# A layer of LayerNorm, S5 scan and gated MLP, re-tiled into four 512-token chunks and ordered by a list scheduler inside the kernel

## The chip, the cores and the metric

One core of a Trainium2 chip. Times are device microseconds (us) of one execution. The kernel before takes 243.13 us (median of two runs, 241.75 to 244.52). A profiled execution gives a *span*, from the first to the last instruction. Engines: PE (TensorE, with its weight loads as PEld), DVE (VectorE), ACT (ScalarE), POOL (GpSimd), and SP, which here only issues DMAs.

## The reference

```python
def reference(A_x, A_Lambda_re, A_Lambda_im, A_B_re, A_B_im, A_C_re, A_C_im, A_log_dt, A_Dskip,
              B_x, B_w_gate, B_w_up, B_w_down):
    x  = A_x                                   # (1, 2048, 448), bfloat16
    xn = _layernorm(x)                         # no scale, no shift
    s  = S5(xn)                                # Bu = xn B_bar^T (complex); h_t = Lam_bar h_{t-1} + Bu_t
                                               # s = 2 Re(h C^T) + xn * Dskip ;  448 states
    g  = silu((sigmoid(xn Wg) * (xn Wu)) Wd)   # 448 -> 1792 -> 448
    return x + s * g
```

(The scan runs over all 2048 tokens.) The feature size 448 is 3 x 128 + 64. TensorE contracts over up to 128 rows, so every contraction over 448 features has a piece of 64 rows. Two 64-row matmuls can run side by side, one in the upper and one in the lower half of the array: a *pair*.

## The kernel before

Tokens are taken in chunks of up to 512 (the first and the last are of 256). Each gate/up unit of 128 hidden features does three full 128-row matmuls for the gate, three for the up half, and one pair for the two 64-row rests. So the array changes its tiling mode in each unit. ScalarE takes the two 512-column PSUM banks out by one instruction each.

```python
def unit_mms(banks, n, xnT, fulls, halves, half_first):
    ...
    def do_full():
        for i in range(nb):
            for kt in range(KF):                       # KF = 3, 128 rows each
                nc.tensor.matmul(banks[i][:, 0:n], lhsT=fulls[i](kt), rhs=xnT[:, kt, 0:n], ...)
    def do_half():
        for i in range(nb):
            lo = H if (i == 1 and ROWPAIR) else 0      # H = 64: upper or lower half of the array
            nc.tensor.matmul(banks[i][:, 0:n], lhsT=halves[i], rhs=xnT[lo:lo + H, 3, 0:n], ...)

def gu_unit(c, xnT, ft, half_first):
    ...
    nc.scalar.activation(sig[:, 0:n], gu[:, 0, 0:n], ACT.Sigmoid)
    nc.scalar.copy(out=ub[:, 0:n], in_=gu[:, 1, 0:n])
    nc.vector.tensor_tensor(out=hF, in0=sig[:, 0:n], in1=ub[:, 0:n], op=ALU.mult)
```

All large loads are issued by SP; ACT issues three tiny ones. B and C are transposed by PE, x of the first chunks by PE and of the later ones by DMA. The order of the instructions is written by hand ("weave" and "slots").

## Time and profile before

| | before |
|---|---|
| timed, median | 243.13 us |
| profiled span | 238.9 us |
| busy PE / DVE / ACT / POOL | 204.5 / 179.4 / 127.4 / 36.3 us |
| first gate/up matmul | 10.85 us |

The page's busy times and its slices (each digit is a fortieth of the span, in tenths busy; PEclk is the granted TensorE clock in tenths, so 5 is half speed and 9 is full; GB/s is what the DMA engines moved):

```profile
PE 204.5 (86%) x1146; PEld 98.1 (41%) x1160; DVE 179.4 (75%) x444; ACT 127.4 (53%) x254; POOL 36.3 (15%) x102
PE   7589538697974999989739999999999999999990
PEclk9889955999998999999959999999999999999997
GB/s 133 351 277 272 348 27 0 4 0 0 44 23 25 0 19 0 0 44 22 22 41 0 25 0 19 0 65 1 19 19 3 19 0 19 22 21 21 22 0 40
```

What PE waited for (engine, tile, line, what released it: us in total, times, longest):

```profile
PE bu L425 <- DMA xnT<-xn: 10.1, 2, 5.7
PE tpx L226 <- DVE xn L211: 8.9, 6, 4.9
```

PE is the engine that sets the time: 86% busy, and solid in the last third. The losses are in the first two thirds: waits for the transposed normalised x (`xnT`, `xn`), and after each wait the clock digit 5, in which the same work takes twice as long.

### The profile page before, as it was taken

Reading aid. Unit: us, or ns where it says so; the run is one execution under the profiler, and the core shown is the slowest. Engines: PE = TensorE matmul, PEld = TensorE weight load, DVE = VectorE, ACT = ScalarE, POOL = GpSimd, SP = SyncE. Lnnn points to the kernel's source line nnn. Section 1 sums busy time; section 2 is a strip of 40 time slices with the busy share of each in tenths; the row PEclk is TensorE's granted clock in tenths of the full one; section 3 lists DMA queues with packets and bytes.
Section 4 is the critical chain, followed back from the end, with each engine's and each line's share of the span. In section 5 each row is a group of like instructions: output and inputs, shape, how many; then the busy total and the mean of one; then the engine's idle time right before and its main releaser. Section 6 shows DMA issues by size and latency. Waiting matters only on the chain.

```text
span 238.9 us, 3346 instructions
## 1 busy us (share of the span) xinstructions
PE 204.5 (86%) x1146; PEld 98.1 (41%) x1160; DVE 179.4 (75%) x444; ACT 127.4 (53%) x254; POOL 36.3 (15%) x102
## 2 busy tenths in 40 slices
PE   7589538697974999989739999999999999999990
PEld 2246316343431444433314444344444455555550
DVE  7999179998799999999995792799666369533204
ACT  3468713478891736676703563874546273533232
POOL 2010720482000068830000000000000000000000
PEclk9889955999998999999959999999999999999997
DMA  6999900000211000011110000020000000000001
GB/s 133 351 277 272 348 27 0 4 0 0 44 23 25 0 19 0 0 44 22 22 41 0 25 0 19 0 65 1 19 19 3 19 0 19 22 21 21 22 0 40
DMA packets 15608, 11.75 MB, mean 49 GB/s; under 512 B 6083, under 2 KB 14662, under 8 KB 15590
## 3 DMA queue, kind: packets, MB, share of 16 engines
q1 hardware_dynamic: 15536, 11.41, 17.2%
q0 software_dynamic: 48, 0.11, 0.4%
q8 instruction: 9, 0.15, 0.3%
q14 instruction: 9, 0.07, 0.1%
q10 hardware_dynamic: 6, 0.00, 0.0%
HBM read 8.37 MB, written 1.84 MB: 43 GB/s over the span
## 4 chain that ended last, share of the span: by engine, by line
PE 48%; DVE 28%; DMA 10%; ACT 5%; POOL 3%; issue 3%; SPq 2%; DVEq 0%; POOLq 0%
PE gu L419 16%; PE acc L586 14%; PE acc L594 6%; DVE wv L517 6%; DMA wk<-in_B_w_gate_dram 5%; PE bu L419 5%; PE gu L425 3%; DMA bc<-in_A_C_im_dram 3%; DMA xnT<-xn 2%; DVE z L510 2%; DVE ta L506 2%; DVE hF L456 2%; DVE tb L508 1%; DVE hT L536 1%; DVE td L534 1%
## 5 line engine op out<-in xcount | busy, mean ns | idle before, releaser
L451 ACT ACTIVATE sig<-gu 128x512 bf16<-128x512 f32 (+1 forms) x56 | 30.4, 543 | 44.8 <-PE gu L425 34.5
L419 PE MATMUL gu<-xnT,wg 128*128 128x512 bf16 (+1 forms) x201 | 47.0, 340 | 2.9 <-ACT ub L455 1.2
L419 PE MATMUL gu<-xnT,wu 128*128 128x512 bf16 (+1 forms) x207 | 48.1, 340 | 0.2
L586 PE MATMUL acc<-wd,hF 128*128 128x448 bf16 x224 | 47.4, 357 | 0.9 <-DVE hF L456 0.8
L456 DVE TENSOR_TENSOR hF<-sig,ub 128x512 bf16<-128x512 bf16 (+1 forms) x56 | 21.0, 385 | 22.9 <-ACT ub L455 22.6
L586 PEld LDWEIGHTS <-hF 128*128 128x128 bf16 x224 | 22.3, 99 | 22.8 <-issue 2.0
L455 ACT CAST ub<-gu 128x512 bf16<-128x512 f32 (+1 forms) x56 | 29.6, 528 | 0.0
L419 PEld LDWEIGHTS <-wu 128*128 128x128 bf16 x210 | 20.8, 99 | 16.4 <-DMA wu<-in_B_w_up_dram 0.2
L419 PEld LDWEIGHTS <-wg 128*128 128x128 bf16 x210 | 17.6, 98 | 23.6 <-issue 12.9
L419 PE MATMUL bu<-xnT,bT 128*128 128x512 bf16 (+1 forms) x103 | 23.9, 367 | 0.7 <-ACT bus_606 L476 0.7
L425 PE MATMUL gu<-xnT,wk 64*128 64x512 bf16 (+1 forms) x140 | 21.2, 343 | 1.3 <-DMA wk<-in_B_w_up_dram 0.6
L594 PE MATMUL acc<-cT,hT 128*128 128x448 bf16 x98 | 20.8, 352 | 0.0
L600 ACT ACTIVATE sigd<-acc 128x448 bf16<-128x448 f32 x16 | 8.7, 544 | 16.1 <-PE acc L586 16.1
L425 PE MATMUL bu<-xnT,bT 64*128 64x512 bf16 (+1 forms) x35 | 7.1, 350 | 11.5 <-DMA xnT<-xn 10.1
L419 PEld LDWEIGHTS <-bT 128*128 128x128 bf16 x105 | 9.8, 104 | 13.0 <-issue 7.1
L594 PEld LDWEIGHTS <-hT 128*128 128x128 bf16 x112 | 11.0, 98 | 10.1
L216 POOL COPY xn<-xn 128x64 bf16<-128x64 bf16 x10 | 4.3, 426 | 70.8 <-ACT xn L215 70.8
L604 DVE TENSOR_TENSOR g_t<-zb,sigd 128x448 bf16<-128x448 bf16 x16 | 6.1, 384 | 11.4 <-ACT zb L602 11.4
L425 PEld LDWEIGHTS <-wk 64*128 64x128 bf16 x140 | 5.2, 94 | 14.3 <-issue 12.6
L226 PE MATMUL tpx<-ident,xn 128*128 128x128 bf16 x24 | 3.3, 279 | 8.9 <-DVE xn L211 8.9
L610 DVE TENSOR_TENSOR sg<-acc,g_t 128x448 bf16<-128x448 f32 x14 | 8.6, 618 | 2.6 <-PE acc L594 2.4
L170 DVE BATCH_NORM_STATS2 stats<-x_all 128x6 f32<-128x448 bf16 x16 | 9.7, 608 | 0.0
(269 smaller groups left out, 299.2 us busy)
## 6 DMA issues: line engine op xcount, KB each, us to landing
out_dram<-o_t SPq DMA_DIRECT2D x16, 112.0 KB, 1.7
wd<-in_B_w_down_dram SPq DMA_DIRECT2D x1, 1568.0 KB, 9.3
x_all<-in_A_x_dram SPq DMA_DIRECT2D x3, 448.0 KB, 7.8
wg<-in_B_w_gate_dram SPq DMA_DIRECT2D x1, 960.0 KB
wu<-in_B_w_up_dram SPq DMA_DIRECT2D x1, 960.0 KB, 11.1
wg<-in_B_w_gate_dram SPq DMA_DIRECT2D x1, 384.0 KB, 5.5
wu<-in_B_w_up_dram SPq DMA_DIRECT2D x1, 384.0 KB, 6.4
bc<-in_A_B_re_dram SPq DMA_DIRECT2D x1, 336.0 KB, 10.7
```

The lines of the kernel that those rows point to most:

```text
L170: nc.vector.bn_stats(out=stats[:], in_=x_all[:, t0 + i, :])
L419: nc.tensor.matmul(banks[i][:, 0:n], lhsT=fulls[i](kt), rhs=xnT[:, kt, 0:n], start=(kt == 0 and not half_first), stop=(kt == KF - 1 and ha ...
L425: nc.tensor.matmul(banks[i][:, 0:n], lhsT=halves[i], rhs=xnT[lo:lo + H, 3, 0:n], start=half_first, stop=not half_first)
L451: sg_ins = nc.scalar.activation(sig[:, 0:n], gu[:, 0, 0:n], ACT.Sigmoid).ins
L455: nc.scalar.copy(out=ub[:, 0:n], in_=gu[:, 1, 0:n])
L456: anchors["hF"] = nc.vector.tensor_tensor(out=hF, in0=sig[:, 0:n], in1=ub[:, 0:n], op=ALU.mult).ins
L517: V.tensor_tensor_scan(out=cell["wv"][:, k, 0:n], data0=rb, data1=cell["z"][:, k, 0:n], initial=(st[pt][:, k, :] if c else 0.0), op0=ALU.m ...
L586: nc.tensor.matmul(dacc[:, 0:D], lhsT=hFs[c][:, ft, j * P:(j + 1) * P], rhs=wd[:, ft, :], start=(ft == 0), stop=(ft == FT - 1))
L594: nc.tensor.matmul(y[:, 0:D], lhsT=hTs[c][:, hm, j * P:(j + 1) * P], rhs=K["cT"][:, cm, :], start=False, stop=(i == 6))
L600: nc.scalar.activation(sigd[:], dacc[:, 0:D], ACT.Sigmoid, scale=half)
L604: nc.vector.tensor_tensor(out=g_t[:], in0=zb[:], in1=sigd[:], op=ALU.mult)
L610: nc.vector.tensor_tensor(out=sg[:], in0=y[:, 0:D], in1=g_t[:], op=ALU.mult)
```

## The change

A rewrite. Its intent: every contraction over 448 features of gate and up becomes seven 64-row pairs, upper half into one PSUM bank and lower half into another, with no full 128-row matmul between, so a step of 14 matmuls has one tiling mode and fills two banks that ScalarE takes out with one 1024-column instruction. There are four chunks of 512 tokens. B, C and the later x chunks are transposed by DMA. And the program order of every engine comes from a small list scheduler in the kernel (`Plan`), which is given an estimated cost for each instruction and each DMA.

```diff
+class Plan:                       # list scheduler; runs while the kernel is built
+    def solve(self, pe_from):
+        ...                       # latest start of each op, backward from PE's order
+            pick = min((x for x in lst if x[0] <= s + 1e-9), key=lambda x: (x[1].late, x[1].idx))
+            ...
+            if o.dma:             # one queue for each issuing engine, 200 GB/s
+                q = dma_free[e] = max(dma_free.get(e, 0.0), o.end + 1.2) + o.dma / 200e3
+                o.lat = q + 0.6 - o.end
...
-    unit_mms((gu[:, 0, :], gu[:, 1, :]), n, xnT, ..., half_first)    # 6 full matmuls and a pair
+        for s in range(7):                                           # 7 pairs
+            T.matmul(gu[a][:, 0, ts], lhsT=w_[0:H, s, ms], rhs=x[0:H, s, ts], ...)
+            T.matmul(gu[a][:, 1, ts], lhsT=w_[H:P, (s + 1) % 7, ms], rhs=x[H:P, s, ts], ...)
...
+    add("ACT", act(1024), lambda: A.activation(sig[b][:], gu[a][:], ACT.Sigmoid), ...)   # two banks at once
...
+    load_w("ACT", "g", 1, 0)                  # half of the weight blocks, issued by ACT
+    load_w("SP", "g", 0, 0)
+    ...
+    load("ACT", "wd", F * D * 2, wd[:], ...)  # ACT also issues the down weights
+    load_x(8, 8, "ACT")                       # and the second half of x
...
+    def chain(t0, n):                         # 1/std of two x tiles; tiles 4 to 15 on GpSimd
+        e, en, c = (V, "DVE", 0.08) if t0 < TPC else (G, "POOL", 0.35)
+        add("POOL", 0.35, lambda: G.tensor_tensor(out=sd, in0=ve, in1=bc(halfc), op=ALU.pow), ...)
...
+    def tload(keys, o, i, nbytes, r=(), chain=True):          # DMA transposes, on SP
+        add("SP", 1.2, lambda: Q.dma_start_transpose(out=o, in_=i), r=r, w=keys, dma=nbytes * 2, chain=chain)
```

## The prediction

> **What bounds the kernel now.** TensorE. The engine totals give PE 204.5 us of a 238.9 us span (86%), DVE 179.4, ACT 127.4; the chain that ended last is 48% PE. In the slices PE is solid from 133 us to the end, at full clock. The losses lie earlier. The waits list: 10.1 us for DMA transposes of xn (two stalls), 8.9 us for xn tiles (4.9 of it behind a GpSimd chain near 30 us). The timeline: first gate/up matmul at 10.9 us; after idle stretches the granted clock falls (0.55 in 30-40 us, 0.67 in 120-130 us) and a 512-column matmul takes 0.43 us instead of 0.215. After PE's last matmul come 5.9 us. The timed median is 4.2 us above the profiled span.
>
> **What stays.** The matmul columns. From the timeline a 512-column matmul costs 0.215 us, a 448-column one 0.189, two concurrent 64-row matmuls (a pair) about 0.22. After the change: 392 gate/up pairs 84.7 us, B 21.2, down 42.4, y with its diagonal skip 25: 173 us, the floor.
>
> **What it removes (estimates from these durations).** (1) Half of some 45 round trips between full and 64-row matmuls, about 0.1 us each way: 4 us. (2) 60 PE transposes of B and C, 6 us at low clock; DMA transposes instead. (3) The GpSimd chain ahead of chunk 1 and the two late DMA transposes, with the cold clock after them: 20 us; normalisation now goes early. (4) ACT evacuates 1024 columns in 1.0 us instead of 2 x 0.54; DVE loses the skip product and the short chunks. I count DVE 154 us, ACT 117; neither is the bound. (5) Tail 1.5 us (last y split).
>
> **What it adds.** ACT now issues twelve loads before its first evacuation, on the eight completion lanes it shares with SP; the instruction order shows its last one waiting for a late weight block. About 3.5 to 4 MB must land first, at the 270 to 350 GB/s of the slices: ACT is free at 13 to 15 us, and the first gate/up matmul comes at 14 to 16 us, cold. Chunk 0's up half is evacuated by DVE from PSUM, about 1.2 us a step against PE's 1.51, while tables, statistics and scans share DVE; in-order queues planned from estimated times will stall a few us there.
>
> **Sum.** Start 15 + PE 173 + mode changes 5 + small matmuls and remaining transposes 2 + cold clock 2 + stalls 5 + tail 4 = 206 us span; plus 4 is about 209 us.
>
> I predict 209 us, 8 in 10 between 200 and 221; faster by over 2% 0.95, within 2% 0.03, slower 0.02.
>
> **What would show it.** PE waits for DMA transposes near zero; PE slices at 9 from about 45 us on, clock 1.0; pairs spaced 0.215 to 0.22 us over a whole step (1.51 us); DVE near 155, ACT near 117 us busy; the first gate/up matmul later than before, waiting for an ACT copy behind its DMA issues. TensorEngine Tiling (Trainium skill, Key Properties) says that changing the tiling mode drains the engine and that tiles load weights in parallel: the 0.1 us gaps agree; long pair runs are not in this trace.
>
> **What would make it wrong.** If long runs of pairs don't hide their weight loads (94 ns each, two per 0.216 us), 392 pairs at 0.25 us cost 13 us more. If the planned orders fit badly, chunks 0 and 1 stall 10 us or more. If ACT isn't held by its DMA issues, about 200 us.

## The result, and the profile after

The changed kernel takes **222.66 us** (222.56 to 222.76, two runs), against 243.13: ratio 0.923, 95% interval 0.914 to 0.933. Run again later, six times beside eleven runs of the kernel before, it took 222.70 us (222.36 to 223.89), ratio 0.921 [0.919, 0.924]. (A ratio is the mean time of one kernel's fast runs over that of the other's of the same rounds, so not quite the ratio of the medians quoted.) Executions over 1.5% slower than the fastest of the same kernel are left out of the means. Both kernels are correct. The direction was right; 222.7 lies above the range of 200 to 221.

The page's busy times and slices of the changed kernel:

```profile
PE 189.1 (85%) x1409; PEld 92.5 (42%) x1416; DVE 160.2 (72%) x301; ACT 112.6 (51%) x155; POOL 42.6 (19%) x97
PE   7200999999899999196999299999999999999993
PEclk9755699999999999979999769999999999999998
GB/s 146 213 235 291 355 128 86 84 163 6 1 0 0 3 0 0 25 84 59 1 24 41 28 96 65 0 21 0 24 0 21 3 0 1 44 22 41 3 15 69
```

Its list of PE's waits:

```profile
PE gu L607 <- DMA wU<-in_B_w_up_dram: 13.0, 1, 13.0
PE gu L607 <- ACT sig L625: 4.7, 1, 4.7
PE gu L660 <- ACT ub L635: 3.6, 1, 3.6
```

PE has 15 us less work and the stretches of half clock in the middle have mostly gone. But in place of the old losses stand an empty stretch at the start (slices of 5.55 us; digits 2, 0, 0) and two holes near 90 and 123 us.

And the timeline of PE inside a step (start us, us, what), where the prediction was right: pair follows pair at 0.21 to 0.22 us (two of a step's seven pairs are shown), though each matmul needs its own weight load.

```profile
32.97 0.38 PE L607 MATMUL gu<-xnT,wG 64*128 64x512 bf16 x1
32.98 0.38 PE L608 MATMUL gu<-xnT,wG 64*128 64x512 bf16 x1
33.19 0.38 PE L607 MATMUL gu<-xnT,wG 64*128 64x512 bf16 x1
33.19 0.38 PE L608 MATMUL gu<-xnT,wG 64*128 64x512 bf16 x1
```

The spans can be split into five terms. The floor is the number of matmul columns times the trace's spacing (392 gate/up pairs at 0.216, 224 down matmuls at 0.189, B 21.2, y 25 us); "busy over the floor" is what PE does besides: tiling-mode changes, transposes, small matmuls, half-clock work, counted from the first gate/up matmul on.

| us | before | after | predicted |
|---|---|---|---|
| first gate/up matmul | 10.9 | 22.0 | 15 |
| floor | 173 | 173 | 173 |
| PE idle from there to its last matmul | 24.5 | 12.8 | 5 |
| PE busy over the floor | 24.7 | 10.4 | 9 |
| tail after the last matmul | 5.9 | 3.8 | 4 |
| span | 238.9 | 222.0 | 206 |

So the 17 us won are +14.3 (less overhead on PE), +11.7 (less idle), +2.1 (tail), and -11.1 (the start). Of the 16 us that are missing against the prediction, 7.0 are at the start, 7.8 are idle time in the middle, 1.4 the rest of the overhead, less 0.2 at the tail.

**The start.** One row of SP and the timeline of ACT in the changed kernel. SPq and ACTq rows are DMA issues; the number after the name of a unit is the idle time before it and what ended it:

```profile
9.82 0.60 SPq L288 DMA_DIRECT2D wG<-in_B_w_gate_dram  x1
10.83 0.63 ACTq L288 DMA_DIRECT2D wd<-in_B_w_down_dram  x1
19.11 0.40 ACTq L288 DMA_DIRECT2D x_all<-in_A_x_dram  x1
19.54 1.28 ACT L406 ACT_TABLE_LOAD   x1 [19.54 <-DMA wU<-in_B_w_up_dram]
20.83 1.07 ACT L406 COPY xnT<-acc 128x512 bf16<-128x512 bf16 x2
```

ACT has nothing to do with weights, and yet it stood for 8 us between two DMA issues. The trace's semaphores show why: the DMAs of SP and ACT share eight completion semaphores in turn, and the issue at 19.11 us waits for the one that the gate-weight block issued by SP at 9.82 us holds; the last part of that block arrived at 19.09 us. Behind that issue in ACT's queue stand its first table load and the copy of the first transposed x, which PE's first gate/up matmul needs. The waits list blames a DMA of up-weights for PE's 13.0 us. It is not even the block that ACT waited for, and the weights were only ACT's obstacle, not PE's.

**The holes.** The timeline of POOL, then of ACT, ahead of the hole at 89.8 to 94.5 us (x2 rows hold two instructions; two rows of POOL's chain are left out):

```profile
81.70 0.92 POOL L358 CAST varb<-mv 128x2 bf16<-128x2 f32 x2 [21.55 <-DVE mv L348]
83.82 2.81 POOL L361 TENSOR_TENSOR sdb<-veb,halfc 128x2 bf16<-128x2 bf16 x2
86.61 2.11 POOL L364 TENSOR_TENSOR rsd<-sdb,negc 128x2 f32<-128x2 bf16 x2
90.16 0.79 POOL L369 TENSOR_SCALAR nmr<-nmr 128x2 f32<-128x2 f32 x2
```

```profile
84.09 0.54 ACT L794 ACTIVATE zb<-acc 128x448 bf16<-128x448 f32 x1
90.80 2.71 ACT L382 ACTIVATE xn<-x_all,nmr,rsd 128x448 bf16<-128x448 bf16 x4 [6.18 <-POOL nmr L369]
93.42 1.00 ACT L625 ACTIVATE sig<-gu 128x1024 bf16<-128x1024 f32 x1
```

GpSimd needs 9.2 us for the statistics of four x tiles. ACT's next instruction is the normalisation of those tiles, which is not urgent, and behind it stands the gate's eviction, which is: PE waits for it. The planner had booked 0.35 us for each of these GpSimd instructions. The power operation (`sdb`, `rsd`) takes 0.70 us when DVE is idle (the one at 23.5 us) and up to 1.58 us here. The Trainium skill, GPSIMD Engine Reference, Specifications, says that GpSimd's SBUF interfaces are shared with VectorE, with contention beside VectorE instructions that have two SBUF inputs or run in a two-port mode. The trace agrees: beside VectorE's scan and its products of two SBUF tiles the operation took 0.71 to 1.61 us, while beside an eviction, which reads one input from PSUM, it took 0.70 and 0.72 us (at 30.0 and 32.6 us) though VectorE was busy throughout. But no run here varied DVE's load alone.

### The profile page after: what moved, and what is told of

Read it like the earlier page. It is cut to its first block, busy times and chain, and to the rows that moved or that the text cites. A ratio compares the mean times of both kernels' runs of the same rounds, so it can differ in the third digit from the quotient of the medians.

```text
span 222.0 us, 3617 instructions
## 1 busy us (share of the span) xinstructions
PE 189.1 (85%) x1409; PEld 92.5 (42%) x1416; DVE 160.2 (72%) x301; ACT 112.6 (51%) x155; POOL 42.6 (19%) x97
## 4 chain that ended last, share of the span: by engine, by line
PE 47%; DVE 25%; DMA 9%; POOL 8%; ACT 5%; issue 3%; SPq 0%; ACTq 0%; DVEq 0%; POOLq 0%
PE gu L607 17%; PE acc L785 10%; PE acc L813 7%; DMA wG<-in_B_w_gate_dram 5%; PE gu L785 5%; DMA wU<-in_B_w_up_dram 4%; PE gu L670 4%; DVE wv L724 3%; DVE hF L631 3%; POOL sdb L361 2%; POOL rsd L364 2%; DVE bst L347 2%; DVE hF L636 2%; ACT ub L635 2%; DVE hT L741 1%
## 5 line engine op out<-in xcount | busy, mean ns | idle before, releaser
L607 PE MATMUL gu<-xnT,wG 64*128 64x512 bf16 (+1 forms) x210 | 48.1, 367 | 15.4 <-DMA wU<-in_B_w_up_dram 13.0
L607 PE MATMUL gu<-xnT,wU 64*128 64x512 bf16 (+1 forms) x203 | 49.3, 382 | 4.7 <-ACT sig L625 4.7
L608 PE MATMUL gu<-xnT,wU 64*128 64x512 bf16 (+1 forms) x203 | 49.3, 383 | 0.0
L608 PE MATMUL gu<-xnT,wG 64*128 64x512 bf16 (+1 forms) x210 | 48.2, 367 | 0.0
L785 PE MATMUL acc<-wd,hF 128*128 128x448 bf16 x168 | 34.6, 359 | 0.0
L607 PEld LDWEIGHTS <-wG 64*128 64x128 bf16 x210 | 19.4, 95 | 24.5 <-issue 4.4
L607 PEld LDWEIGHTS <-wU 64*128 64x128 bf16 x203 | 19.2, 97 | 23.4 <-issue 3.1
L625 ACT ACTIVATE sig<-gu 128x1024 bf16<-128x1024 f32 x21 | 21.5, 1022 | 14.6 <-PE gu L608 14.6
L635 ACT CAST ub<-gu 128x1024 bf16<-128x1024 f32 x21 | 21.2, 1010 | 13.8 <-PE gu L608 13.7
L636 DVE TENSOR_TENSOR hF<-sig,ub 128x1024 bf16<-128x1024 bf16 x21 | 14.3, 682 | 14.9 <-ACT ub L635 14.8
L608 PEld LDWEIGHTS <-wG 64*128 64x128 bf16 x210 | 19.2, 95 | 13.9 <-issue 13.9
L724 DVE TENSOR_TENSOR_SCAN wv<-c_r,st,z 128x512 bf16<-128x512 f32 x18 | 22.9, 1280 | 0.2
L608 PEld LDWEIGHTS <-wU 64*128 64x128 bf16 x203 | 19.2, 97 | 5.0 <-issue 5.0
L670 PE MATMUL gu<-xnT,bT 128*128 128x512 bf16 x65 | 16.4, 399 | 1.3 <-issue 1.3
L813 PEld LDWEIGHTS <-hT 128*128 128x128 bf16 x119 | 10.4, 98 | 7.3 <-issue 0.4
```

Source lines behind the costliest of these rows:

```text
L607: T.matmul(gu[a][:, 0, ts], lhsT=w_[0:H, s, ms], rhs=x[0:H, s, ts], start=(s == 0), stop=(s == 6))
L608: T.matmul(gu[a][:, 1, ts], lhsT=w_[H:P, (s + 1) % 7, ms], rhs=x[H:P, s, ts], start=(s == 0), stop=(s == 6))
L625: add("ACT", act(1024), lambda: A.activation(sig[b][:], gu[a][:], ACT.Sigmoid), r=[("gu", a), "sinL", "cosL", "sth", "cth"] + [(s, p) for ...
L635: add("ACT", act(1024), lambda: A.copy(out=ub[b][:], in_=gu[a][:]), r=[("gu", a)], w=[("ub", b)])
L636: add("DVE", dve2(1024), lambda: V.tensor_tensor(out=ho, in0=sig[sb_][:], in1=ub[b][:], op=ALU.mult), r=[("sig", sb_), ("ub", b)], w=hk)
L670: T.matmul(gu[a][:, i, :], lhsT=bT[:, kt, i, pt * P:pt * P + P], rhs=x[:, 2 * kt, :], start=False, stop=(kt == 2))
```

## The experiments

Theory A: the 11 us lost at the start are ACT's held queue. Theory B: the holes come from an order that was planned with wrong GpSimd durations. The rival to both, theory D: VectorE is so full (0.98 busy from 40 to 80 us in the windows of the changed kernel) that whatever is repaired, PE will wait for VectorE's results instead.

### e1_act_free: ACT issues two loads fewer

```diff
-    load("ACT", "wd", F * D * 2, wd[:], B_w_down.rearrange("(ft p) d -> p ft d", p=P))
-    load_x(8, 8, "ACT")
+    load("SP", "wd", F * D * 2, wd[:], B_w_down.rearrange("(ft p) d -> p ft d", p=P))
+    load_x(8, 8)
```

> Only change: the load of w_down and the load of x tiles 8 to 15 are issued by SP behind the B transposes instead of by ACT ahead of its first evacuation. Theory A (ACT was held at the head of its queue by a DMA issue that waited for a late weight block): the first ACT copy starts near 12 us instead of 20.8, the first gate/up matmul near 12 to 13 us instead of 22.0, and the time falls by 7 to 10 us to about 213 to 216 us, with the two GpSimd stalls unchanged. Rival B (the weights themselves were late, as the wait list names a DMA of w_up): the first gate/up matmul stays near 20 us or PE stalls on weights for as long right after, and the time falls by less than 2 us.

212.72 us (212.28 to 213.12), ratio 0.881 [0.877, 0.885]; span 211.3. The first gate/up matmul moves from 21.95 to 12.48 us, ACT's table load from 19.54 to 10.06 us. That is theory A. The gate block landed when it had before (its last part at 18.95 us, against 19.09), so the gain is the queue's and not that of earlier weights. The holes at 90 and 123 us are gone without anything having been done to GpSimd, but a new and longer one has appeared. Waits of PE, then ACT's timeline:

```profile
PE gu L657 <- ACT ub L635: 9.3, 1, 9.3
```

```profile
47.75 1.02 ACT L625 ACTIVATE sig<-gu 128x1024 bf16<-128x1024 f32 x1
56.15 1.24 ACT L761 COPY wv<-wv 64x512 bf16<-64x512 bf16 x2 [7.38 <-DVE wv L756]
57.41 1.01 ACT L635 CAST ub<-gu 128x1024 bf16<-128x1024 f32 x1
```

Again an instruction of ACT that nobody hurries for (a copy of half a scan result) stands in front of an eviction that PE needs, and waits 7.4 us for a scan that VectorE has not reached.

### e2_pool_cost: only the planner's estimates of GpSimd

```diff
-        e, en, c = (V, "DVE", 0.08) if t0 < TPC else (G, "POOL", 0.35)
+        e, en, c = (V, "DVE", 0.08) if t0 < TPC else (G, "POOL", 0.6)
+        cp = 0.35 if t0 < TPC else 1.4          # booked for the two pow instructions
```

> Only numbers of the planner change: GpSimd statistics operations of tiles 4 to 15 are planned at 0.6 us (was 0.35), the two pow operations at 1.4 us (was 0.35), as measured under DVE load. No instruction is added or removed; orders change. Theory A (the plan puts the GpSimd chain too late, so ACT's in-order queue stands behind the normalisation): the PE waits of 4.7 and 3.6 us and the half-clock matmuls after them go, 8 to 11 us less, about 212 to 215 us; start still at 22 us. Rival B (these waits come from ACT or DVE being overloaded there, not from the chain's place): similar waits of several us come back elsewhere, and the time changes by less than 3 us.

209.3 us (209.09 to 213.03), ratio 0.867 [0.862, 0.872]; span 207.4. No instruction was added, removed or made faster; only the order changed. It is lower than the 212 to 215 us that I had expected. The start is as late as ever (21.7 us), and after it PE hardly waits: 0.5 us is the longest. The first row of its waits; the first and last row of POOL's chain for two tiles of chunk 2; then the last row of its chains for chunk 3, and ACT's rows beside it:

```profile
PE gu L608 <- ACT xnT L407: 13.2, 2, 12.7
```

```profile
83.72 0.55 POOL L359 CAST varb<-mv 128x2 bf16<-128x2 f32 x1 [16.44 <-DVE mv L348]
86.94 0.23 POOL L370 TENSOR_SCALAR nmr<-nmr 128x2 f32<-128x2 f32 x1
122.41 1.79 POOL L370 TENSOR_SCALAR nmr<-nmr 128x2 f32<-128x2 f32 x2
122.22 1.01 ACT L636 CAST ub<-gu 128x1024 bf16<-128x1024 f32 x1 [2.17 <-PE gu L609]
123.13 1.41 ACT L383 ACTIVATE xn<-x_all,nmr,rsd 128x448 bf16<-128x448 bf16 x2
```

For chunk 2 the planner, with honest estimates, no longer interleaves two chains: a pair of tiles is through in 3.4 us (83.72 to 87.17), where the changed kernel needed 9.2 us for two pairs and released neither before the end. For chunk 3 it still interleaves them, and they take 8.2 us (115.96 to 124.20). Yet nothing waits there, because the eviction `ub` now stands ahead of the normalisation in ACT's order. So it is the place of the normalisation, more than the length of the chain, that made the holes. Theory B holds, and this one group of estimates is worth 13.4 us.

### e3_both: both edits together

> Both edits together. If the two losses are independent, the gains add: 15 to 20 us, about 203 to 207 us. If the later start had hidden work that is still needed (B transposes, tables, coefficients), new PE waits of several us for bT or cT appear in 30 to 60 us and the sum falls short by that much.

211.57 us (210.83 to 213.18), ratio 0.876 [0.871, 0.881]: worse than e2 alone, and 5 us above the 203 to 207 that I had expected of independent gains. The first gate/up matmul is at 12.6 us, some nine earlier than in e2, and those nine are lost again: in waits for ACT's copies (bus 2.8, ub 2.3, sig 1.1 us) and for transposes (2.1), and at a clock of 0.77 to 0.89 in the windows around them. Two repairs worth 10 and 13.4 us alone are worth 11.1 together. This was the case for theory D.

### e4_chain4: the GpSimd chain in two groups of four

e1_act_free, with the chains of tiles 8 to 15 made shorter in fact and not only in the plan:

```diff
-        if t % 2 == 1:
+        if t < 8 and t % 2 == 1:
             chain(t - 1, 2)
+        elif t % 4 == 3:
+            chain(t - 3, 4)
```

> The first edit (loads off ACT), and the GpSimd chain for tiles 8 to 15 in two groups of four instead of four groups of two, planned costs as they were: half as many GpSimd operations. If an operation's time is nearly all fixed cost (0.60 us for 128x1, 0.70 for 128x2), the chain takes about half as long (9 us to 5), each of the two stalls falls by 3 us or more, and the time lies 5 to 9 us below that of the first edit alone. If the time goes with the elements, there is no gain over the first edit.

210.56 us (210.44 to 210.85), ratio 0.872 [0.868, 0.876]. I had expected 5 to 9 us under e1_act_free; it is 2.2. A pow over four columns took 1.0 to 1.3 us here, where one over two took 0.7 to 1.6 in the changed kernel; the chain for chunk 2 took 4.8 us (71.36 to 76.13), against 8.9 for the two chains of e1 (69.92 to 78.81). But the 9.3 us wait for the eviction `ub`, now PE's longest, stands as in e1.

### e5_sp and e5_cols: relieving VectorE

e5_sp is e3_both with fewer loads issued by ACT (its four vectors first, then only the first weight blocks). e5_cols does in addition the small computation of the scan's columns, on which VectorE's sine tables depend, before the x transposes and not after chunk 0's first steps, so that VectorE works in the early time in which it had been idle:

```diff
     warm_mm(5)
+    columns()
     for t in range(4):
         stats(t)
 ...
         gu_evac(0, k, m, a)
-    columns()
     tables()
```

> e3_both, and of the weights ACT issues only the first block's lower halves, behind the four small vectors; SP issues the rest in fewer, larger transfers (blocks of 2 and 5 instead of 2, 2 and 3). ACT is then free near 5 us. Theory: the first gate/up matmul is no longer bound by ACT's issues but by the x chain, near 9.5 to 10.5 us (12.5 in e1_act_free). But DVE is already behind (0.99 busy from 27 us on), so PE will only wait longer for it in 40 to 70 us: time about that of e3_both, within 2 us of 211. If PE's start alone decides, 208 to 209 us.

> e5_sp with the parameter columns made on PE before the x transposes instead of after the first three gate/up steps, so that the 8 us of table work on DVE and the sines on ACT can run in DVE's idle time before 20 us. If DVE's backlog is what PE waits for in 40 to 70 us, PE waits after the start fall to under 4 us and the time to 200 to 204 us. If it isn't, the time stays within 2 us of e5_sp.

e5_sp 216.05 us (213.07 to 216.66), ratio 0.886 [0.875, 0.896]. e5_cols 209.17 us (208.17 to 210.23), ratio 0.863 [0.854, 0.871]. Both missed what I had expected: e5_sp lies 5 us above e3_both and not within 2 us of 211, and e5_cols is neither at 200 to 204 us nor within 2 us of e5_sp. The two longest waits of PE in e5_sp:

```profile
PE gu L655 <- ACT sig L623: 8.6, 1, 8.6
PE gu L655 <- DVE bT L550: 5.9, 1, 5.9
```

In e5_cols the second is 1.8 us. So of the 4.9 us between the two traced runs (213.07 and 208.17) 4.1 are this wait, for a copy (`bT`) that VectorE made behind its table work: there theory D was right. But the first, of 8.6 us, was in both, identical, although VectorE began the scan in question at 55.63 us in one and at 50.95 in the other. ACT's timeline in e5_cols, and SP's row for the eight transposes of chunk 1's x:

```profile
41.27 1.02 ACT L620 ACTIVATE sig<-gu 128x1024 bf16<-128x1024 f32 x1 [1.25 <-PE gu L606]
52.20 1.24 ACT L759 COPY wv<-wv 64x512 bf16<-64x512 bf16 x2 [9.91 <-DVE tq L730]
```

```profile
29.91 11.26 SPq L306 DMA_TRANSPOSE xnT<-xn  x8
```

Chunk 1's x had been issued by 41.2 us (a transpose takes 2.4 us to land: page, DMA issues), and PE began chunk 1 at 42.5 us; three steps later it stood, because no eviction had freed a PSUM slot. I then printed what the kernel's own planner had assumed when it chose the order. It had booked that x as landing at 51.6 us, and PE as idle from 42.2 to 51.6. In such a gap it costs nothing, on paper, to put the two scan copies ahead of the first gate eviction. The cause of the booking is one line: each DMA transpose is booked with twice its bytes at 200 GB/s in a queue of its engine, behind every load of that queue, and moving loads from ACT to SP (e1, e3, e4, e5) lengthened that queue. The plan of e1_act_free has the same gap, from 36.8 to 45.8 us; the plans of the changed kernel and of e2, where ACT's queue carried those loads, have none there. I had therefore not repaired ACT's queue only; each time, I had also made the planner believe in a 9 us pause. Theory P: the new hole is made by the order, not by VectorE's load.

### e6_land: one number of the planner

```diff
-  tload([k + ("a",)], xnT[c % 3][:, 0:7:2, js], xn[b][:], P * 1024, ...)
-  tload([k + ("b",)], xnT[c % 3][:, 1:6:2, js], xn[b][:, 64:448], P * 768, ...)
+  tload([k + ("a",)], xnT[c % 3][:, 0:7:2, js], xn[b][:], 1, ...)
+  tload([k + ("b",)], xnT[c % 3][:, 1:6:2, js], xn[b][:, 64:448], 1, ...)
```

(The fifth argument is the bytes booked; the transfer is the same.)

> One number of the planner is changed against e5_cols: the bytes that it books for the SBUF-to-SBUF transposes of the normalised x (it booked them twice over at 200 GB/s, so that chunk 1's x was planned to land at 51.6 us; in the e5_cols trace it was issued from 29.9 to 41.2 and landed about 43.6). No instruction is added or removed, only the order on DVE, ACT, POOL and SP may change. Theory P (the order was made for a landing that never happened: ACT's two stack copies were placed ahead of the first gate eviction of chunk 1 because the plan saw idle time there): the 8.6 us wait of PE for the sig eviction at 50 to 58 us goes to under 2 us; the plan itself now leaves 4.4 us before chunk 2 (84 to 88 us), so a wait of 0 to 4 us there; 201 us, 198 to 205. Theory D (DVE is simply behind with its work between 33 and 60 us): 5 us or more of wait stay at 45 to 60 us under another name; 206 to 210 us.

205.46 us (204.41 to 208.11), ratio 0.847 [0.843, 0.851]; span 203.6. The 8.6 us wait is gone. What PE waits for now, and the same place in ACT's timeline:

```profile
PE gu L605 <- DMA xnT<-xn: 4.5, 2, 3.9
```

```profile
45.70 1.02 ACT L623 ACTIVATE sig<-gu 128x1024 bf16<-128x1024 f32 x1
52.97 0.62 ACT L759 COPY wv<-wv 64x512 bf16<-64x512 bf16 x1
```

The scan copies now come after the gate eviction. The 3.9 us wait is ahead of chunk 2, where the new plan itself left 4.4 us: its GpSimd estimate (1.4 us for every pow) was now too high. The time lies half a microsecond above the range that I had written for theory P and half a microsecond under theory D's; the place of the waits decides for P.

### e7_four and e8_x23: the next terms in the plan

e7_four groups the chains as e4_chain4 did and gives the planner their measured durations. e8_x23 also loads x tiles 2 and 3 ahead of the weights and keeps the transposes of all chunks in program order in the plan.

```diff
 e7:     e, en, c = (V, "DVE", 0.08) if t0 < TPC else (G, "POOL", 0.45)
 e7:     cp = 0.7 if t0 < TPC else 1.25
 e8:     load_x(1, 1)
 e8: +   load_x(2, 2)
```

> e6_land with the GpSimd chains of tiles 8 to 15 in two groups of four, and the planner given their durations from the e4_chain4 trace (small ops 0.45, pow 1.25 us). Theory P: the wait before chunk 2's first pair that e6_land's plan has goes; 198 to 202 us, 1 to 4 us under e6_land. If GpSimd is no longer on the path in e6_land, the same as e6_land within 1 us.

> e7_four with tiles 2 and 3 of x loaded ahead of the weight blocks, and all chunks' DMA transposes kept in program order in the plan. In e5_cols DVE waited 2.9 us until 9.6 us for these tiles and chunk 0 ran at a granted clock of 0.83 between 10 and 20 us. Expected: x tiles 2 and 3 land before 6 us, the first gate/up pair stays at 9.5 to 11 us, the clock between 10 and 20 us rises above 0.9, 1.5 to 3 us under e7_four: 196 to 200 us. If the weight block was what the start waits for, the first pair comes 1 us later and the gain is under 1 us.

Both came out inside their ranges. e7_four 201.92 us (200.6 to 203.47), ratio 0.835 [0.830, 0.840]. e8_x23 **199.06 us** (198.29 to 199.46), ratio **0.822** [0.819, 0.825], correct; it is 11% under the changed kernel (0.822 over 0.921 is 0.892). In e8 the first gate/up matmul comes at 9.14 us and the clock is full from 10 to 20 us. Each of the two makes two changes at once, and which of them gains how much was not separated. Its page and the longest of its waits:

```profile
PE 184.6 (94%) x1409; PEld 90.4 (46%) x1416; DVE 159.2 (81%) x301; ACT 111.9 (57%) x155; POOL 38.5 (20%) x85
PE   6898778998999999999999999999999999999991
```

```profile
PE gu L655 <- DVE bT L550: 1.8, 1, 1.8
```

PE is the whole story: 94% busy. VectorE's work is the same as in the changed kernel (159.2 against 160.2 us), and from 40 to 80 us VectorE is again 0.98 busy while PE is 0.97 busy, so theory D as I had stated it, that the work itself would not fit, is wrong.

### e12_land4: the same one number, in the simpler base

e4_chain4 with e6's edit alone. Here PE's and GpSimd's orders are unchanged.

> e4_chain4 (210.6 us; a 9.3 us wait of PE at 50 to 59 us for the ub eviction, ACT standing at the stack copies) with the one planner number of e6_land, the booked bytes of the x transposes. TensorE's and GpSimd's orders are the same, only DVE, ACT and SP orders change. The plan of e4_chain4 had idle PE from 36.8 to 45.8 us ahead of chunk 1, the new plan has none. Theory P (order planned for a landing that does not happen): the 9.3 us wait goes to under 2 us, 202 to 206 us. Theory D (DVE backlog after the earlier start): 5 us or more of waits stay between 45 and 75 us, 207 us or more.

207.16 us (205.61 to 208.21), ratio 0.854 [0.851, 0.858], 3.4 us under e4_chain4 (its four runs scatter over 2.6 us, and the record classes it as unclear, but each lies under all four of e4_chain4). The 9.3 us wait at 50 to 59 us became 0.5 us, as theory P says. But only 3.4 of the 9.3 us arrived: a wait for transposes of 3.3 us came before chunk 2, and the clock fell to 0.66 between 90 and 100 us. Its rows:

```profile
PE gu L607 <- DMA xnT<-xn: 3.5, 2, 3.3
PE gu L657 <- ACT ub L635: 0.5, 1, 0.5
```

The total misses my range and falls into theory D's; the location of the waits does not. The 9.3 us hole was the plan's. For the new wait, hold the plan against the trace: PE was ready for chunk 2 at 87.6 us, 8.4 later than planned, and VectorE's statistics of its tiles were done at 73.1, 9.1 later; so VectorE adds 0.7 us at most. The GpSimd chain took 4.6 us where 2.1 were booked (e12 keeps the old 0.35), and the eight transposes held SP 11.8 us where 9.6 were booked. That points to further wrong bookings more than to theory D, but none of them was varied alone here; e7_four books the chain better, and its waits for transposes are 1.8 us in all.

### e9_warm and e10_warm60: what the cold clock of chunk 0 costs

More warm-up matmuls in front of the changed kernel's first gate/up matmul, while PE would be idle; the plan is told that they are free.

```diff
+    add("PE", 0.01, lambda: [T.matmul(gu[2][:, 0, :], lhsT=warm[:, 0:P], rhs=warm[:], start=True, stop=True)
+                             for _ in range(36)], r=["warm"], w=[("gu", 2)])        # e10: 60
```

> The changed kernel with 36 more warm-up matmuls (512 columns, data that is there from the start) between the first two x transposes and the first gate/up pair, planned as free, so no order changes elsewhere: it prices the cold clock of chunk 0 alone. Theory: the first gate/up pairs at 22 us run at 0.215 us instead of 0.42 us, the granted clock between 20 and 26 us is above 0.9, and the time falls by 1.5 to 2.5 us (220.2 to 221.2 us). If chunk 0 there waits for DVE or ACT evictions rather than for PE's clock, the pairs get short but the time stays within 0.7 us of 222.7.

> e9_warm sized right: its 36 extra matmuls ended at 16.4 us and PE then stood idle for 6.1 us, so chunk 0 was cold all the same. 60 of them (8.2 us for 36 in e9_warm, so 13.7 us) reach from 8.2 us to about 22 us, where the changed kernel's first gate/up pair waits for ACT's table load and xnT copy. Theory: the pairs at 22 to 25 us are spaced 0.11 us (256 columns) instead of 0.21 us, and the time falls by 1 to 2 us against the changed kernel's 222.7 (so 220.7 to 221.7). If the evictions or the x tiles 2 and 3 set the pace of chunk 0, the pairs get short but the time stays within 0.7 us of 222.7.

e9_warm 223.17 us (222.75 to 223.72), ratio 0.922 [0.920, 0.925]: a badly sized experiment. Its 36 matmuls ended at 16.4 us, PE then idled for 6.1 us and was as cold as before. e10_warm60 kept the granted clock at 1.0 over the first 30 us, and its first pairs came every 0.11 us (256 columns) and not every 0.21. It took 223.07 us (222.42 to 224.5), ratio 0.922 [0.917, 0.927]: no gain that the timing can see. In the trace the hole of 4.7 us ended at 93.80 us against 94.47, so 0.7 us was won by then. But the warm-ups ran too long this time: the first pair came at 22.88 us, 0.93 later than in the changed kernel. In e9_warm, as cold as before, a start 0.57 later ended the hole 0.61 later. So my estimate is that the cold clock of chunk 0 costs about 1.6 us in the trace (0.7 and 0.9); neither run shows a gain in the total.

### e11_modes: what a change of tiling mode costs

e8_x23 with B's order pair 0, full 0, pair 1, full 1 in place of pair 0, pair 1, full 0, full 1: the same instructions, 16 more changes of mode.

> e8_x23 with the order inside each pair of B units changed: pair 0, full 0, pair 1, full 1 in place of pair 0, pair 1, full 0, full 1. The same instructions, 16 more changes of the tiling mode; the order on the other engines is the same. If a change of mode costs 0.1 us as I counted in the prediction (45 round trips of 0.2 us), the time rises by 1.6 us over e8_x23's 199.1, to 200.2 to 201.2 us, and PE's gaps at the B units grow by that. If a change costs nothing that shows, 199.1 within 0.6 us.

I wrote there that the other engines' order is the same. It is not: the planner shifted some neighbours on the other four engines. 199.14 us (198.42 to 200.4), ratio 0.823 [0.818, 0.828]: not distinguishable from e8_x23, and below the 200.2 that I expected. The trace is finer than the clock on the wall. A stretch of B units in e8_x23, from its first pair to the first down matmul (the row x5 lacks one record):

```profile
102.94 0.38 PE L655 MATMUL gu<-xnT,bT 64*128 64x512 bf16 x1
103.16 0.27 PE L658 MATMUL gu<-xnT,bT 64*128 64x256 bf16 x1
103.59 1.24 PE L668 MATMUL gu<-xnT,bT 128*128 128x512 bf16 x5 [0.16 <-issue]
105.32 2.81 PE L783 MATMUL acc<-wd,hF 128*128 128x448 bf16 x14
```

and in e11_modes:

```profile
102.93 0.38 PE L655 MATMUL gu<-xnT,bT 64*128 64x512 bf16 x1
104.64 0.28 PE L658 MATMUL gu<-xnT,bT 64*128 64x256 bf16 x1
105.52 2.81 PE L783 MATMUL acc<-wd,hF 128*128 128x448 bf16 x14
```

2.38 us became 2.59: one more round trip, 0.21 us, and the same 0.21 at two other undisturbed places (0.11 at a third). The Trainium skill, TensorEngine Tiling, Key Properties, says that a change of tiling mode drains the engine; the trace agrees, with 0.1 us a change. Eight round trips would be 1.7 us; the profiled span grew by 0.5, since in two other places, in chunk 1, PE had short waits in e8_x23 (0.67 and 0.46 us of gaps) that e11_modes did not have.

### e13_after: the changed kernel again

> The changed kernel as it is, for its number beside more runs of the kernel before and beside e12_land4 on the same chip: 222.7 within 0.7 us, ratio 0.92.

222.70 us, as quoted above.

## Why the prediction was right or wrong

**Right: what bounds, and the floor.** PE bounds before and after. Pairs run at 0.215 us over whole steps with their weight loads hidden; DVE came to 160.2 us (predicted 154), ACT to 112.6 (117), the tail to 3.8 (4).

**Right: what PE no longer does.** PE's busy time over the floor fell by 14.3 us to 10.4; predicted 9 (mode changes 5, small matmuls 2, cold clock 2). Counted in the traces, the changes of mode between gate, up, B and down matmuls fell from 90 to 30; at 0.1 us, which e11's trace confirms, that is near 6 us, where I had put 4. PE transposes fell from 84 to 28 in the traces; those of B and C had cost 7.6 us (3.3, 2.7 and 1.6), where I had put 6.

**Wrong in size: "Start 15".** The mechanism was named exactly ("the instruction order shows its last one waiting for a late weight block"), and e1 shows that it is the cause: without the two loads the start moves to 12.48 us. The term was mis-sized: the start came at 21.95, 7.0 us later. I divided the bytes that must land by the rates in the full slices of the kernel before (270 to 350 GB/s) and got 13 to 15 us for ACT to be free. The bytes were right and the rate was not: by 19.1 us the changed kernel had moved 4.0 MB, 211 GB/s on average (its slices: 146, 213, 235, 291), and even the kernel before, whose first slice ran at 133, had its first 4.0 MB only at 15.7 us. Why the changed kernel is slower still was not tested. ACT was free at 19.5, and from there it was 2.4 us to the first pair, not 1: a table load (1.28 us), two copies by ACT (1.07) and one by DVE.

**Wrong: "stalls 5", and behind it "normalisation now goes early".** PE idled 12.8 us after its start, 7.8 more than predicted. Normalisation was planned early, but its GpSimd chain was late (9.2 us for what the plan had booked at 0.35 us an instruction), and an in-order ACT carried the lateness to PE. The place was wrong too: I had put the stalls into chunk 0, where VectorE evicts; the two holes, 4.7 and 3.6 us, came at the end of chunk 1 and in chunk 2. I had listed the danger ("If the planned orders fit badly", for chunks 0 and 1) and left it out of the sum. e2 shows the size: the booked durations alone cost 13.4 us.

**"Cold clock 2" was no error that mattered.** e10 takes the cold start of chunk 0 away, which is worth about 1.6 us in the trace by the estimate above and nothing measurable in time.

**"Plus 4" was wrong, and by luck it hid part of the miss.** I took the 4.2 us between the median and the span of the kernel before, which are of different executions; in one and the same execution the difference is 1.7 to 1.8 us. The span was missed by 16 us, the time only by 13.7.

**"If ACT isn't held by its DMA issues, about 200 us" was wrong as it stood.** e1 gave 212.7. The gain was 10 us, not 22, because the planner answered the move of two loads with a worse order. e6 and e12 show that answer to be one booked number; about 200 us needed, besides, better GpSimd durations, grouped chains, VectorE's table work moved forward and x loaded earlier (e8: 199.1).

What stays open: why the changed kernel's first loads were slower; what the median of e5_sp, 3 us above its traced run, hides; and how much of the long pow times is VectorE's interference. None was isolated.

## What to carry to other kernels

A planned order is only as good as its estimates, and on engines that work in order one late, unimportant instruction ahead of an urgent one costs the whole difference; so compare the plan's times with the trace's before explaining a wait by load. After any edit of an auto-ordered kernel, look at what the planner made of it: a repair can be paid back by an order chosen for a pause that never comes. And don't let an engine that evicts PSUM issue large loads late in a row of them: its compute stands behind its own DMA issues.

## What the Trainium skill lacked or had wrong

- **DMA: Bandwidth & Descriptors**, section "Issuing engines are not separate DMA queues", says that issuing from several engines saves only the sequencer's time, usually little. It doesn't say what that can cost: ACT's issues held its compute queue until 19.5 us, with one issue 8.3 us after the one before (10.83, 19.11); with two loads moved to SP, ACT was free at 10.06 us and the kernel took 212.7 in place of 222.7 us.
- **DMA: Bandwidth & Descriptors** gives bandwidths for DMA transposes. Of the time that the issuing queue is held it has only sequencer cycles in a table about a later chip and its predecessors, and none for a transfer of this size on this chip. Here eight SBUF-to-SBUF transposes held SP for 11.26 us (1.4 us each), landing 2.4 us after issue; for a planner these two numbers matter, not the bytes.
- **GPSIMD Engine Reference** has no duration for the power operation on small tiles: 0.70 us (two columns, DVE idle), up to 1.61 us under DVE load; for four columns 1.01 us with DVE idle (e4_chain4) and up to 1.97 (e8_x23). Its remark on shared SBUF interfaces fits, without a size.
- **TensorEngine Tiling**, Key Properties, names the drain at a change of mode without a size: 0.21 us for a round trip here. It says that tiles load weights in parallel, but not whether a long run of 64-row pairs hides a weight load for each matmul: it does, at 0.215 us for 512 columns.
- **TensorE: Matmul & The Clock Gate**, section "Wait — 56ns, not 53.3ns?", gives start-to-start times of 215.7 ns warm and 426.7 ns cold for 512 columns; the trace agrees (0.215 and 0.42 us), also for pairs. Nothing to mend there.
